# The first feature unit of two token groups by eight plain block products, half of the tokens at a time, with early loads

## Chip, cores, metric

One core of one Trainium2 chip. The metric is the device time of one execution in microseconds (us); lower is better. Ratios are the mean time of one kernel's fast runs over that of the other's fast runs of the same rounds, so not quite the ratio of the medians that are quoted beside them.

In the lines of the profile PE is TensorE's products, DVE is VectorE, ACT ScalarE, POOL GpSimd, and SPq the issue of a load. L315 is a line of that run's kernel file (each run has its own numbering), x8 a count of instructions. A wait reads: who waited <- for what: sum, times, longest (us). Of the tiles, `x` is the output of attention, `st` a state, `w` (before: `win`, `wout`) weights, `d` the banks of the plain products, `A_h` to `D_h` and `A_o` to `D_o` those of the hidden and the output products.

## The reference

```python
# attention: B=4, H=8, S=768, D=64; gamma_h = 1 - 2^(-5-h)
for t in range(S):
    state = gamma * state + outer(k[:, :, t], v[:, :, t])
    y[:, :, t] = q[:, :, t] @ state / sqrt(D)
# bridge: (B,H,S,D) -> x of 3072 tokens x 512
h = x @ w_in                      # 512 x 2048, float64 weights
out = maximum(0.01 * h, h) @ w_out    # 2048 x 512
```

The kernel handles the sequence in six groups `c` of 128 positions x 4 batches (512 tokens). Attention within a group is done by products (scores `ap`, masked `am`, values `yp`, state sums). The two large products use the seven-product scheme of Winograd on 2 x 2 blocks, over four "units" `u` of 512 hidden features. The weights come as float64 and are turned into float32 in 32 "pieces": ScalarE takes the powers, VectorE the mantissas.

## The kernel before

What the change and the argument touch (cuts marked):

```python
def sums(w):                     # weight sums of a unit: 4 VectorE operations
def differences(x, t):           # differences of x: 4 VectorE operations
...
PRODUCTS = {"M1": ("A", 0, 0), "M6": ("B", 5, 5), "M5": ("C", 4, 4), "M4": ("D", 3, 6),
            "M2": ("A", 2, 2), "M7": ("B", 1, 1), "M3": ("C", 6, 3)}
def seven(tiles, name, takes, order=...):   # 7 block products, each 4 matmuls
...                                         # (8 instructions in the trace)
load(0, 0); nc.sync.dma_start(out=dec, in_=decay)
load_piece(0); load_piece(1); load(0, 1); load_piece(2)
...                    # later heads are loaded into a ring of two, when the head two before is done
for b in range(B):                # group 0: four heads, then differences and sums
    scored(0, b)(); round_piece(); read(0, b)()
all_of(differences(*xs[0]), sums(win[0]))
for u in range(NU):
    for c in range(2):
        ...
        if (c, u) == (0, 0):      # two heads of group 1 beside group 0's products
            at = put(rounds(1), s0=[scored(1, 0)], s2=[read(1, 0)], s3=[scored(1, 1)], s5=[read(1, 1)])
        elif (c, u) == (1, 0):    # the other two with nothing beside them
            for b in range(2, B):
                scored(1, b)(); round_piece(); read(1, b)()
            differ(1)()
        run(hidden(c, u, *xs[c], *parts[c][1:], **order), at)
    for c in range(2):
        run(output(c, os[c], [parts[c]], u == 0, u == NU - 1), at)
```

Of the kernel before, what the change touches and what calls it, by code (L numbers as in the profile page):

```python
# [9 lines left out]
FP32 = mybir.dt.float32  # L10
# [8 lines left out]
C = 128  # L19
# [4 lines left out]
def kernel(  # L24
# [52 lines left out]

    win = [const.tile([128, 7, 2, 256], FP32, name=f"win{u}") for u in range(NU)]
    wout = [const.tile([128, 7, 2, 256], FP32, name=f"wout{u}") for u in range(NU - 1)]

    st = [const.tile([128, HP, D], FP32, name=f"st{b}") for b in range(B)]

    last_s4 = const.tile([128, 1, 2, 256], FP32, name="last_s4")
    if f64:
        last = []
    else:
        last = [const.tile([128, 2, 2, 256], FP32, name=f"last{h}") for h in range(3)]

    def block(w, i):

        if w is not last:
            return w[:, i]
        return w[i // 2][:, i % 2] if i < 6 else last_s4[:, 0]
# [9 lines left out]
    def load(c, b):  # L103
        x = work.tile([128, 2, HP, C], FP32, tag="qk", bufs=AHEAD, name=f"qk_{c}_{b}")
        y = work.tile([128, 2, H, D], FP32, tag="kv", bufs=AHEAD, name=f"kv_{c}_{b}")
        nc.sync.dma_start(out=x, in_=qk[c, b])
        nc.sync.dma_start(out=y, in_=kv[c, b])
        heads[c, b] = x, y
# [24 lines left out]
    def stage_y(c, bs, xb):  # L133
# [24 lines left out]
        for b, _, _, _, ps in got:  # L158
            th, o = divmod(b * C, N)
            blocks = xb.rearrange("p (kh th) k n -> p kh th k n", th=2)[:, :, th, :, ds(o, C)]  # L160
            nc.vector.tensor_tensor(out=blocks, in0=ps[:, :, 0 : HP // 2, :], in1=gq, op=ALU.mult)  # L161
            sp = sums[b]
            if more:
                if c > 0:
                    nc.vector.tensor_tensor(out=st[b], in0=st[b], in1=sp, op=ALU.add)
                nc.vector.tensor_tensor(out=st[b], in0=st[b] if c > 0 else sp,
                                        in1=gc.unsqueeze(2).to_broadcast([128, HP, D]),
                                        op=ALU.mult)
            n = c * B + b + AHEAD
            if n < NC * B and n - 2 * B not in range(AHEAD):  # L170
                load(*divmod(n, B))


    wout.append(last)
    units = [w for pair in zip(win, wout) for w in pair]
    N_PIECES = 4 * len(units)
    raws = {}
    done = [0]
# [4 lines left out]
    def piece(n):  # L183

        w, h, i = units[n // 4], n // 2 % 2, n % 2
        return w[h][:, :, i, :] if w is last else w[:, 2 * h : 2 * h + 2, i, :]

    def load_piece(n):
        if n >= N_PIECES:
            return  # L190
        if not f64:
            nc.sync.dma_start(out=piece(n), in_=weights[n].rearrange("p (h n) -> p h n", h=2))
            return
        tag, bufs = ("raw", 3) if n < N_PIECES - 4 else (("qk", "kv")[n % 2], AHEAD)
        raws[n] = work.tile([128, W], I64, tag=tag, bufs=bufs, name=f"raw{n}")
        nc.sync.dma_start(out=raws[n], in_=weights[n])

    def new_last(h):
        if f64 and len(last) == h:
            last.append(work.tile([128, 2, 2, 256], FP32, tag="raw", bufs=3, name=f"last{h}"))  # L200

    def round_piece():

        n = done[0]
        done[0] += 1
        if f64:
            mantissas(n)
        load_piece(n + 3)
        if n + 2 < N_PIECES and f64:
            powers(n + 2)  # L210
        if n == N_PIECES - 1:
            new_last(2)
            for b in range(AHEAD):
                load(2, b)
        if n % 4 == 3 and n > 3:
            all_of(sums(units[n // 4]))
# [3 lines left out]
    def powers(n):  # L220




        if n >= N_PIECES - 4:
            new_last(n // 2 % 2)
        top = raws[n].bitcast(U16).rearrange("p (h n four) -> p h n four", four=4, h=2)[:, :, :, 3]
        z = zs[n] = work.tile([128, 2, W // 2], I16, tag="z", bufs=3, name=f"z{n}")
        x = piece(n)


        nc.scalar.activation(x, top, AF.Prelu, alpha=float(BEND), scale=1.0 / 16,
                             bias=-7.5 / 16 - TOP)
        nc.scalar.activation(z, x, AF.Prelu, alpha=1.0 / BEND, bias=-float(BEND))
        nc.scalar.activation(z.bitcast(U16), z, AF.Relu, scale=128.0, bias=32768.0)
# [21 lines left out]
    def sums(w):  # L257

        a11, a21, a12, a22, s1, s2, s4 = (block(w, i) for i in range(7))
        plus(s1, a21, a22)  # L260
        yield
        minus(s2, s1, a11)
        yield
        minus(a21, a11, a21)
        yield
        minus(s4, a12, s2)
        yield

    def differences(x, t):

        minus(t[:, 0], x[:, 1], x[:, 0])
        yield
        minus(t[:, 1], x[:, 3], t[:, 0])
        yield
        minus(t[:, 2], x[:, 2], t[:, 1])
        yield
        minus(x[:, 1], x[:, 3], x[:, 1])
        yield

    def all_of(*steps):  # L280

        for _ in zip(*steps):
            pass


    PRODUCTS = {"M1": ("A", 0, 0), "M6": ("B", 5, 5), "M5": ("C", 4, 4), "M4": ("D", 3, 6),
                "M2": ("A", 2, 2), "M7": ("B", 1, 1), "M3": ("C", 6, 3)}

    def seven(tiles, name, takes, order=("M1", "M6", "M5", "M4", "M2", "M7", "M3")):
# [3 lines left out]
        for m in order:  # L293
            bank, sa, sb = PRODUCTS[m]
# [18 lines left out]
    def hidden(c, u, x, t, g, gd, **order):  # L313
# [6 lines left out]
        def takes(m, ps):  # L320
# [20 lines left out]
            elif m == "M3":  # L341
                plus(g[:, 1], got["u2"], ps)
                leaky(1)
                all_of(differences(g, gd))

        return seven([(win[u], x, t)], f"h{at}", takes, **order)

    def output(c, o, parts, first, final):
# [45 lines left out]
        return seven([(wout[u], g, gd) for u, g, gd in parts], f"o{at}", takes)  # L394


    def new_x(c):
        x = work.tile([128, 4, 2, N], FP32, tag="x", bufs=2, name=f"x_{c}")
# [30 lines left out]
    def differ(c):  # L429
        return lambda: all_of(differences(*xs[c]))  # L430
# [12 lines left out]
    load_piece(0)  # L443
    load_piece(1)
    load(0, 1)
    load_piece(2)
# [3 lines left out]
    if f64:  # L450
        powers(0)
        powers(1)

    xs = {}
    os = {}
    xs[0] = new_x(0)
    for b in range(B):
        scored(0, b)()
        round_piece()
        read(0, b)()  # L460
    all_of(differences(*xs[0]), sums(win[0]))


    for u in range(NU):
        parts = []
        for c in range(2):
            parts.append(new_g(c, u))
            order = {}
            at = rounds(1, 3)
            if (c, u) == (0, 0):  # L470
                xs[1] = new_x(1)
                order["order"] = ("M1", "M2", "M6", "M5", "M4", "M7", "M3")
                at = put(rounds(1), s0=[scored(1, 0)], s2=[read(1, 0)], s3=[scored(1, 1)],
                         s5=[read(1, 1)])
            elif (c, u) == (1, 0):
                for b in range(2, B):
                    scored(1, b)()
                    round_piece()
                    read(1, b)()
                differ(1)()  # L480
                at = rounds(1)
            run(hidden(c, u, *xs[c], *parts[c][1:], **order), at)
        for c in range(2):
            if u == 0:
                os[c] = new_o(c)
            at = rounds(1, 4) if u < NU - 1 else {}
            if u == NU - 1 and NC > 2:
# [106 lines left out]
```

## Time and profile before

| | before |
|---|---|
| time, median of 3 (range) | 686.09 us (685.8 to 687.5) |
| profiled execution | span 683.2 us, mean granted TensorE clock 0.995 |
| TensorE busy | 660.3 us, 97% |
| first output product (`A_o`) starts | 74.7 us in the chain |
| TensorE waits in the first 110 us / after | 18.7 us / none |

The lines are in the prediction below. The table is to be read as follows: after the first output product TensorE never waits, so a change in the opening is worth what it moves that start by, and no more.

### The profile page before, as it was taken

How to read it: one execution, taken by the hardware profiler on the slowest of the kernel's cores; microseconds unless marked ns; L12 is line 12 of the kernel's file. 1: busy time of each engine (PE TensorE's matmuls, PEld its weight loads, DVE VectorE, ACT ScalarE, POOL GpSimd, SP SyncE). 2: the span in 40 equal slices, each digit the busy share in tenths (PEclk: the TensorE clock that was granted, in tenths of full speed). 3: DMA queues.
4: the chain of work that ended last, by engine and by line, in shares of the span. 5: the costliest groups of instructions: out<-in, count | busy, mean ns of one | idle time of the engine just before them, and what ended most of it. 6: DMA issues, size and time to landing. Idle time of an engine off the chain costs nothing.

```text
span 683.2 us, 9545 instructions
## 1 busy us (share of the span) xinstructions
PE 660.3 (97%) x4096; PEld 577.8 (85%) x4096; DVE 375.9 (55%) x573; ACT 166.4 (24%) x275; POOL 27.4 (4%) x29
## 2 busy tenths in 40 slices
PE   5787999999999999999999999999999999999997
PEld 5666888888888888888888888888888888888886
DVE  4878767988888765613653533553451354341342
ACT  5422444445543001311210221220221130221210
POOL 1110000000001010100100100100000000000000
PEclk9998999999999999999999999999999999999999
DMA  8741212223412353100301300301300000100001
GB/s 317 284 155 62 86 69 88 91 69 123 153 33 93 127 181 117 71 1 12 112 1 62 124 0 1 124 1 62 124 0 1 1 1 16 46 1 0 1 1 62
DMA packets 15162, 49.12 MB, mean 72 GB/s; under 512 B 1680, under 2 KB 1680, under 8 KB 15120
## 3 DMA queue, kind: packets, MB, share of 16 engines
q1 hardware_dynamic: 15120, 48.51, 20.4%
q8 instruction: 32, 0.52, 0.3%
q14 instruction: 10, 0.08, 0.0%
HBM read 42.21 MB, written 6.29 MB: 71 GB/s over the span
## 4 chain that ended last, share of the span: by engine, by line
PE 94%; DMA 2%; DVE 1%; issue 1%; POOL 0%; SPq 0%; POOLq 0%
PE B_h L303 12%; PE A_o L303 12%; PE B_o L303 12%; PE C_o L303 12%; PE C_h L303 12%; PE A_h L303 12%; PE D_h L303 6%; PE D_o L303 6%; PE ap L126 3%; PE yp L148 3%; PE yp L143 1%; PE yp L155 1%; DMA qk<-in_qk_dram 1%; DMA dec<-decay_dram 1%; DMA kv<-in_kv_dram 1%
## 5 line engine op out<-in xcount | busy, mean ns | idle before, releaser
L303 PE MATMUL A_h<-x,win 128*128 128x256 f32 x384 | 91.0, 380 | 0.0
L303 PEld LDWEIGHTS A_h<-x,win 128*128 128x128 f32 x384 | 72.7, 190 | 10.0
L303 PE MATMUL A_o<-g,wout 128*128 128x256 f32 x288 | 68.2, 380 | 0.0
L318 ACT ACTIVATE g<-g 128x512 f32<-128x512 f32 x72 | 43.8, 630 | 85.3 <-DVE g L252 85.3
L303 PEld LDWEIGHTS A_o<-g,wout 128*128 128x128 f32 x288 | 54.6, 190 | 7.8 <-ACT g L333 0.5
L252 DVE TENSOR_TENSOR m<-m,B_h 128x512 f32<-128x512 f32 x24 | 16.5, 686 | 62.3 <-PE B_h L303 62.3
L323 ACT COPY m<-A_h 128x512 f32<-128x512 f32 x24 | 14.0, 582 | 136.5 <-PE A_h L303 104.1
L252 DVE TENSOR_TENSOR m<-m,B_o 128x512 f32<-128x512 f32 x16 | 11.0, 686 | 65.7 <-PE B_o L303 65.7
L303 PE MATMUL B_h<-t,win 128*128 128x256 f32 x192 | 45.5, 380 | 1.0 <-DVE t L255 1.0
L303 PE MATMUL C_h<-t,win 128*128 128x256 f32 x192 | 46.1, 383 | 0.0
L303 PE MATMUL B_h<-x,win 128*128 128x256 f32 x192 | 46.0, 382 | 0.0
L112 POOL TENSOR_TENSOR kv<-kv,dec 128x512 f32<-128x512 f32 x24 | 26.9, 1122 | 468.1 <-DMA kv<-in_kv_dram 241.0
L303 PE MATMUL D_h<-t,win 128*128 128x256 f32 x192 | 45.5, 380 | 0.0
L303 PE MATMUL C_h<-x,win 128*128 128x256 f32 x192 | 45.5, 380 | 0.0
L161 DVE TENSOR_TENSOR x<-yp,dec 128x512 f32<-128x512 f32 x24 | 16.5, 687 | 48.6 <-PE yp L155 36.3
L303 PEld LDWEIGHTS B_h<-t,win 128*128 128x128 f32 x192 | 36.4, 190 | 6.3 <-DVE t L255 1.4
L303 PEld LDWEIGHTS D_h<-t,win 128*128 128x128 f32 x192 | 36.4, 190 | 5.0
L303 PEld LDWEIGHTS C_h<-x,win 128*128 128x128 f32 x192 | 36.4, 190 | 5.0
L303 PEld LDWEIGHTS C_h<-t,win 128*128 128x128 f32 x192 | 35.9, 190 | 5.4
L303 PEld LDWEIGHTS B_h<-x,win 128*128 128x128 f32 x192 | 36.0, 190 | 5.3 <-issue 0.3
L148 PE MATMUL yp<-am,kv 128*64 128x128 f32 x384 | 27.1, 295 | 11.5 <-issue 7.3
L255 DVE TENSOR_TENSOR gd<-g,gd 128x512 f32<-128x512 f32 x48 | 36.4, 758 | 1.6
(88 smaller groups left out, 1004.3 us busy)
## 6 DMA issues: line engine op xcount, KB each, us to landing
raw<-in_weights_dram SPq DMA_DIRECT2D x32, 512.0 KB, 3.9
qk<-in_qk_dram SPq DMA_DIRECT2D x24, 512.0 KB, 4.3
kv<-in_kv_dram SPq DMA_DIRECT2D x24, 512.0 KB, 5.5
out_dram<-o SPq DMA_DIRECT2D x24, 256.0 KB, 2.1
dec<-decay_dram SPq DMA_DIRECT2D x1, 262.0 KB, 5.0
```

The source lines that it names most:

```text
L112: nc.gpsimd.tensor_tensor(out=v, in0=v, in1=gk.unsqueeze(2).to_broadcast([128, H, D]), op=ALU.mult)
L126: nc.tensor.matmul(ps[:, j, a, :], lhsT=x[ts(j, 64), 1, a, :], rhs=x[ts(j, 64), 0, a, :])
L143: nc.tensor.matmul(ps[ts(i, 64), j, m, :], lhsT=st[b][ts(j, 64), a, :], rhs=x[ts(j, 64), 0, a, :], start=(m == 0), stop=False, skip_group_ ...
L148: nc.tensor.matmul(ps[ts(i, 64), j, m, :], lhsT=y[:, 1, 2 * a + j, :], rhs=am[:, j, a, :], start=(c == 0 and m == 0), stop=True, skip_grou ...
L155: nc.tensor.matmul(sp[ts(j, 64), a, :], lhsT=y[:, 0, 2 * a + j, :], rhs=y[:, 1, 2 * a + j, :], start=False, stop=True, skip_group_check=True)
L161: nc.vector.tensor_tensor(out=blocks, in0=ps[:, :, 0 : HP // 2, :], in1=gq, op=ALU.mult)
L252: nc.vector.tensor_tensor(out=out, in0=a, in1=b, op=ALU.add)
L255: nc.vector.tensor_tensor(out=out, in0=a, in1=b, op=ALU.subtract)
L303: nc.tensor.matmul(ps[:, i, :], lhsT=block(w, sa)[:, k, ts(i, 128)], rhs=rhs[:, k, :], start=(first and i == 0 and n == 0 and k == 0), sto ...
L318: nc.scalar.activation(g[:, i], g[:, i], AF.Prelu, alpha=0.01)
L323: nc.scalar.copy(out=got["m1"], in_=ps)
```

## The change

Intent: with plain products a half of the tokens can start as soon as its two heads and two weight pieces are there, without sums of weights or differences of x. More heads are loaded from the start, into tiles whose own contents come later. Core of the diff:

```diff
+    def direct(c, u, x, g, th):          # 8 products of a group, in two halves of tokens th
+        banks = [psum.tile(...) for r in range(2)]
+        for kh in range(2):
+            for r in range(2):
+                for i in range(2):
+                    for k in range(2):
+                        nc.tensor.matmul(banks[r][:, i, :],
+                            lhsT=block(2 * u, r + 2 * kh)[:, k, ts(i, 128)],
+                            rhs=x[:, 2 * kh + th, k, :], ...)
+                if kh == 1:
+                    nc.scalar.activation(g[:, 2 * r + th], banks[r], AF.Prelu, alpha=0.01)
+                yield
...
+    load_piece(3, tile_x("words")...)
+    load(0, 2, new_o("in2"))
+    load(0, 3, new_o("in3"))
+    load(1, 0, unit_tile(LATE[2], "in10"))
+    load(1, 1, unit_tile(LATE[1], "in11"))
...
-    for b in range(B):
-        scored(0, b)()
-        round_piece()
-        read(0, b)()
-    all_of(differences(*xs[0]), sums(win[0]))
+    scored(0, 0)(); read(0, 0)(); scored(0, 1)(); next_mantissas(); next_powers()   # lines joined, some calls left out
+    read(0, 1)(); next_mantissas()
+    run(direct(0, 0, ..., 0), {1: [next_mantissas, next_mantissas, scored(0, 2)], 3: [scored(0, 3)]})
+    load(1, 2, unit_tile(LATE[0], "in12")); load(1, 3)
+    read(0, 2)(); read(0, 3)()
+    run(direct(0, 0, ..., 1), {1: [scored(1, 0)], 3: [scored(1, 1)]})
+    read(1, 0, 1)(); next_mantissas(); next_mantissas()
+    run(direct(1, 0, ..., 0), {1: [scored(1, 2)], 3: [scored(1, 3)]})
+    differences(*parts[0][1:]); read(1, 2, 3)(); next_mantissas()
+    run(direct(1, 0, ..., 1), {0: [next_mantissas]})
...
+            if u == 0:                        # moved: differences of x, weight sums of unit 0
+                put(at, s2=[differ(c)])
+                if c == 0:
+                    put(at, s3=[lambda: add_sums(0)])
```

I call the four calls of `direct` the half groups A, B (group 0) and C, D (group 1).

More of the change, by code (lines that the diff above doesn't have):

```diff
@@ L75, with unit_tile, new_pair, unit @@
     dec = const.tile([128, HP * C + H + HP], FP32, name="dec")
-    win = [const.tile([128, 7, 2, 256], FP32, name=f"win{u}") for u in range(NU)]
-    wout = [const.tile([128, 7, 2, 256], FP32, name=f"wout{u}") for u in range(NU - 1)]
     st = [const.tile([128, HP, D], FP32, name=f"st{b}") for b in range(B)]
+    units = {}
+    N_UNITS = 2 * NU
+    LATE = range(N_UNITS // 2, N_UNITS - 1)
     last_s4 = const.tile([128, 1, 2, 256], FP32, name="last_s4")
-    if f64:
-        last = []
-    else:
-        last = [const.tile([128, 2, 2, 256], FP32, name=f"last{h}") for h in range(3)]
-    def block(w, i):
-        if w is not last:
-            return w[:, i]
-        return w[i // 2][:, i % 2] if i < 6 else last_s4[:, 0]
+    def unit_tile(k, name):
+        if k in LATE:
+            return work.tile([128, 7, 2, 256], FP32, tag=f"late{k}", name=name)
+        return const.tile([128, 7, 2, 256], FP32, name=name)
+    def new_pair(h):
+        pairs = units.setdefault(N_UNITS - 1, [])
+        if len(pairs) == h:
+            pairs.append(work.tile([128, 2, 2, 256], FP32, tag="raw", bufs=3, name=f"last{h}"))
+    def unit(k):
+        if k not in units:
+            units[k] = unit_tile(k, f"w{k}")
+        return units[k]
+    def block(k, i):
+        if k < N_UNITS - 1:
+            return unit(k)[:, i]
+        return units[k][i // 2][:, i % 2] if i < 6 else last_s4[:, 0]
     gq = dec[:, 0 : HP * C].rearrange("p (j m t) -> p j m t", j=2, t=C)
@@ L101, with load @@
     AHEAD = 2
-    def load(c, b):
-        x = work.tile([128, 2, HP, C], FP32, tag="qk", bufs=AHEAD, name=f"qk_{c}_{b}")
-        y = work.tile([128, 2, H, D], FP32, tag="kv", bufs=AHEAD, name=f"kv_{c}_{b}")
+    def load(c, b, place=None):
+        if place is None:
+            x = work.tile([128, 2, HP, C], FP32, tag="qk", bufs=AHEAD, name=f"qk_{c}_{b}")
+            y = work.tile([128, 2, H, D], FP32, tag="kv", bufs=AHEAD, name=f"kv_{c}_{b}")
+        else:
+            flat = place.rearrange("p i k n -> p (i k n)")
+            half = 2 * HP * C
+            x = flat[:, 0:half].rearrange("p (s a t) -> p s a t", s=2, a=HP)
+            y = flat[:, half : 2 * half].rearrange("p (s h d) -> p s h d", s=2, h=H)
         nc.sync.dma_start(out=x, in_=qk[c, b])
@@ L169, in stage_y @@
             n = c * B + b + AHEAD
-            if n < NC * B and n - 2 * B not in range(AHEAD):
+            if c > 1 and n < NC * B:
                 load(*divmod(n, B))
-    wout.append(last)
-    units = [w for pair in zip(win, wout) for w in pair]
-    N_PIECES = 4 * len(units)
+    N_PIECES = 4 * N_UNITS
     raws = {}
-    done = [0]
+    done = {"powers": 0, "mantissas": 0}
     TOP = 1151
@@ L183, in piece, with load_piece @@
     def piece(n):
-        w, h, i = units[n // 4], n // 2 % 2, n % 2
-        return w[h][:, :, i, :] if w is last else w[:, 2 * h : 2 * h + 2, i, :]
-    def load_piece(n):
+        k, h, i = n // 4, n // 2 % 2, n % 2
+        if k < N_UNITS - 1:
+            return unit(k)[:, 2 * h : 2 * h + 2, i, :]
+        new_pair(h)
+        return units[k][h][:, :, i, :]
+    def load_piece(n, place=None):
         if n >= N_PIECES:
@@ L193, in load_piece, with next_powers, next_mantissas @@
             return
-        tag, bufs = ("raw", 3) if n < N_PIECES - 4 else (("qk", "kv")[n % 2], AHEAD)
-        raws[n] = work.tile([128, W], I64, tag=tag, bufs=bufs, name=f"raw{n}")
-        nc.sync.dma_start(out=raws[n], in_=weights[n])
-    def new_last(h):
-        if f64 and len(last) == h:
-            last.append(work.tile([128, 2, 2, 256], FP32, tag="raw", bufs=3, name=f"last{h}"))
-    def round_piece():
-        n = done[0]
-        done[0] += 1
+        if place is None:
+            tag, bufs = ("raw", 3) if n < N_PIECES - 4 else (("qk", "kv")[n % 2], AHEAD)
+            raws[n] = work.tile([128, W], I64, tag=tag, bufs=bufs, name=f"raw{n}")
+        else:
+            raws[n] = place.bitcast(I64)
+        nc.sync.dma_start(out=raws[n], in_=weights[n])
+    def next_powers():
+        n = done["powers"]
+        done["powers"] += 1
+        if n < N_PIECES and f64:
+            powers(n)
+    def next_mantissas():
+        n = done["mantissas"]
+        done["mantissas"] += 1
         if f64:
             mantissas(n)
-        load_piece(n + 3)
-        if n + 2 < N_PIECES and f64:
-            powers(n + 2)
+        if n != 3:
+            load_piece(n + 4 if n < 3 else n + 3)
         if n == N_PIECES - 1:
-            new_last(2)
+            new_pair(2)
             for b in range(AHEAD):
@@ L215, in round_piece @@
         if n % 4 == 3 and n > 3:
-            all_of(sums(units[n // 4]))
+            add_sums(n // 4)
+    def round_piece():
+        next_mantissas()
+        next_powers()
     zs = {}
     def powers(n):
-        if n >= N_PIECES - 4:
-            new_last(n // 2 % 2)
         top = raws[n].bitcast(U16).rearrange("p (h n four) -> p h n four", four=4, h=2)[:, :, :, 3]
@@ L255, in minus, with add_sums, seven @@
         nc.vector.tensor_tensor(out=out, in0=a, in1=b, op=ALU.subtract)
-    def sums(w):
-        a11, a21, a12, a22, s1, s2, s4 = (block(w, i) for i in range(7))
+    def add_sums(k):
+        a11, a21, a12, a22, s1, s2, s4 = (block(k, i) for i in range(7))
         plus(s1, a21, a22)
-        yield
+        minus(a21, a11, a21)
         minus(s2, s1, a11)
-        yield
-        minus(a21, a11, a21)
-        yield
         minus(s4, a12, s2)
-        yield
     def differences(x, t):
         minus(t[:, 0], x[:, 1], x[:, 0])
-        yield
         minus(t[:, 1], x[:, 3], t[:, 0])
-        yield
         minus(t[:, 2], x[:, 2], t[:, 1])
-        yield
         minus(x[:, 1], x[:, 3], x[:, 1])
-        yield
-    def all_of(*steps):
-        for _ in zip(*steps):
-            pass
-    PRODUCTS = {"M1": ("A", 0, 0), "M6": ("B", 5, 5), "M5": ("C", 4, 4), "M4": ("D", 3, 6),
-                "M2": ("A", 2, 2), "M7": ("B", 1, 1), "M3": ("C", 6, 3)}
-    def seven(tiles, name, takes, order=("M1", "M6", "M5", "M4", "M2", "M7", "M3")):
+    def seven(tiles, name, takes):
         banks = {}
-        for m in order:
-            bank, sa, sb = PRODUCTS[m]
+        which = [("M1", "A", 0, 0), ("M6", "B", 5, 5), ("M5", "C", 4, 4), ("M4", "D", 3, 6),
+                 ("M2", "A", 2, 2), ("M7", "B", 1, 1), ("M3", "C", 6, 3)]
+        for m, bank, sa, sb in which:
             first = bank not in banks
@@ L311, in temp, with hidden @@
         return work.tile([128, 2, N], FP32, tag=name, name=f"{name}_{at}")
-    def hidden(c, u, x, t, g, gd, **order):
+    def direct(c, u, x, g, th):
+        banks = [psum.tile([128, 2, N], FP32, tag="ff", bufs=4, name=f"d{r}_{c}_{th}")
+                 for r in range(2)]
+        for kh in range(2):
+            for r in range(2):
+                for i in range(2):
+                    for k in range(2):
+                        nc.tensor.matmul(
+                            banks[r][:, i, :], lhsT=block(2 * u, r + 2 * kh)[:, k, ts(i, 128)],
+                            rhs=x[:, 2 * kh + th, k, :], start=(kh == 0 and i == 0 and k == 0),
+                            stop=(kh == 1 and k == 1), skip_group_check=True)
+                if kh == 1:
+                    nc.scalar.activation(g[:, 2 * r + th], banks[r], AF.Prelu, alpha=0.01)
+                yield
+    def hidden(c, u, x, t, g, gd):
         got = {}
@@ L343, in takes @@
                 leaky(1)
-                all_of(differences(g, gd))
-        return seven([(win[u], x, t)], f"h{at}", takes, **order)
+                differences(g, gd)
+        return seven([(2 * u, x, t)], f"h{at}", takes)
     def output(c, o, parts, first, final):
@@ L392, in takes, with tile_x @@
                 store(1)
-        return seven([(wout[u], g, gd) for u, g, gd in parts], f"o{at}", takes)
+        return seven([(2 * u + 1, g, gd) for u, g, gd in parts], f"o{at}", takes)
+    def tile_x(c):
+        return work.tile([128, 4, 2, N], FP32, tag="x", bufs=2, name=f"x_{c}")
     def new_x(c):
-        x = work.tile([128, 4, 2, N], FP32, tag="x", bufs=2, name=f"x_{c}")
+        x = tile_x(c)
         t = work.tile([128, 3, 2, N], FP32, tag="t", bufs=2, name=f"t_{c}")
@@ L429, in differ @@
     def differ(c):
-        return lambda: all_of(differences(*xs[c]))
+        return lambda: differences(*xs[c])
     def put(at, **more):
@@ L442 @@
     nc.sync.dma_start(out=dec, in_=decay)
-    load_piece(0)
-    load_piece(1)
     load(0, 1)
-    load_piece(2)
+    for n in range(3):
+        load_piece(n)
+    load_piece(3, tile_x("words").rearrange("p i k n -> p (i k n)")[:, 0 : 2 * W])
+    load(0, 2, new_o("in2"))
+    load(0, 3, new_o("in3"))
+    load(1, 0, unit_tile(LATE[2], "in10"))
+    load(1, 1, unit_tile(LATE[1], "in11"))
     nc.vector.memset(mask, 1.0)
@@ L449 @@
                             base=0, pattern=[[1, 128]], channel_multiplier=-1)
-    if f64:
-        powers(0)
-        powers(1)
-    xs = {}
+    for _ in range(3):
+        next_powers()
+    xs = {0: new_x(0)}
     os = {}
-    xs[0] = new_x(0)
-    for b in range(B):
-        scored(0, b)()
-        round_piece()
-        read(0, b)()
-    all_of(differences(*xs[0]), sums(win[0]))
+    parts = [new_g(0, 0)]
+    scored(0, 0)()
+    read(0, 0)()
+    scored(0, 1)()
+    next_mantissas()
+    next_powers()
+    read(0, 1)()
+    next_mantissas()
+    run(direct(0, 0, xs[0][0], parts[0][1], 0),
+        {1: [next_mantissas, next_mantissas, scored(0, 2)], 3: [scored(0, 3)]})
+    load(1, 2, unit_tile(LATE[0], "in12"))
+    load(1, 3)
+    read(0, 2)()
+    read(0, 3)()
+    run(direct(0, 0, xs[0][0], parts[0][1], 1), {1: [scored(1, 0)], 3: [scored(1, 1)]})
+    next_powers()
+    next_powers()
+    xs[1] = new_x(1)
+    parts.append(new_g(1, 0))
+    read(1, 0, 1)()
+    next_mantissas()
+    next_mantissas()
+    run(direct(1, 0, xs[1][0], parts[1][1], 0), {1: [scored(1, 2)], 3: [scored(1, 3)]})
+    next_powers()
+    next_powers()
+    differences(*parts[0][1:])
+    read(1, 2, 3)()
+    next_mantissas()
+    run(direct(1, 0, xs[1][0], parts[1][1], 1), {0: [next_mantissas]})
+    next_powers()
+    next_powers()
+    differences(*parts[1][1:])
     for u in range(NU):
-        parts = []
-        for c in range(2):
+        for c in range(2) if u > 0 else ():
+            if c == 0:
+                parts = []
             parts.append(new_g(c, u))
-            order = {}
-            at = rounds(1, 3)
-            if (c, u) == (0, 0):
-                xs[1] = new_x(1)
-                order["order"] = ("M1", "M2", "M6", "M5", "M4", "M7", "M3")
-                at = put(rounds(1), s0=[scored(1, 0)], s2=[read(1, 0)], s3=[scored(1, 1)],
-                         s5=[read(1, 1)])
-            elif (c, u) == (1, 0):
-                for b in range(2, B):
-                    scored(1, b)()
-                    round_piece()
-                    read(1, b)()
-                differ(1)()
-                at = rounds(1)
-            run(hidden(c, u, *xs[c], *parts[c][1:], **order), at)
+            run(hidden(c, u, *xs[c], *parts[c][1:]), rounds(1, 3))
         for c in range(2):
@@ L486 @@
             at = rounds(1, 4) if u < NU - 1 else {}
+            if u == 0:
+                put(at, s2=[differ(c)])
+                if c == 0:
+                    put(at, s3=[lambda: add_sums(0)])
             if u == NU - 1 and NC > 2:
```

## The prediction

The sum: -1.9 for the start, the moved work and GpSimd, then +0.5 and -0.4, which gives 684.3 us. What is left after the first cut ("the fall", "the return", "the start was slow") is about the granted clock in the profile of the kernel before.

> **What bounds the kernel now.** I read the page first (engine totals and the rows of 40 slices), then TensorE's waits before and after 110 us, then the chain that ended last and the timeline of the first 110 us, then tables by stretch. The page:
>
> ```profile
> PE 660.3 (97%) x4096; PEld 577.8 (85%) x4096; DVE 375.9 (55%) x573; ACT 166.4 (24%) x275; POOL 27.4 (4%) x29
> PE   5787999999999999999999999999999999999997
> ```
>
> TensorE is busy 97% of the span, and each digit covers 17 us: only the first four or five are below 9. So 22.9 us (683.2 less 660.3) are idle, nearly all at the start. The list of TensorE's waits between 110 us and the end is empty; that of the first 110 us holds five rows, sum 18.7 us:
>
> ```profile
> PE yp L148 <- issue: 7.3, 4, 4.6
> PE ap L126 <- DMA qk<-in_qk_dram: 6.2, 3, 4.6
> PE yp L148 <- DVE am L129: 2.7, 2, 1.4
> PE yp L148 <- POOL kv L112: 1.5, 1, 1.5
> PE B_h L303 <- DVE t L255: 1.0, 1, 1.0
> ```
>
> 4.6 us of it is the first load. The rest, 14.1 us, is the attention products waiting for inputs or for VectorE. Idle is not the whole loss. In the chain (start, duration, what) the same work takes two durations:
>
> ```profile
> 8.14 1.97 PE yp L148 x16
> 10.11 0.85 PE yp L155 x16
> 10.97 2.03 PE ap L126 x16
> ...
> 25.35 1.09 PE yp L148 x16
> 26.45 0.47 PE yp L155 x16
> 26.91 1.92 PE A_h L303 x8
> 28.83 1.09 PE ap L126 x16
> ...
> 33.58 0.60 PE yp L143 x16
> ...
> 53.42 1.97 PE yp L148 x16
> ...
> 74.72 1.73 PE A_o L303 x8
> ```
>
> Up to about 17 us and again from 53.4 to 58 us TensorE runs at half speed. The table by stretch shows why in the second case (the number after POOL's is the granted clock):
>
> ```profile
> 49.00:50.00 1.00, 0.00 (x0) 0.00 (x0) 0.97 (x2) 0.94 (x3) 0.00 (x0) 1.00 0.05 20
> 51.00:52.00 1.00, 0.00 (x0) 0.00 (x0) 1.00 (x1) 0.00 (x0) 0.64 (x1) 0.84 0.00 0
> 53.00:54.00 1.00, 0.58 (x6) 0.61 (x8) 0.97 (x3) 0.00 (x0) 0.00 (x0) 0.50 0.00 0
> 58.00:59.00 1.00, 0.98 (x20) 0.56 (x16) 0.69 (x1) 0.97 (x2) 0.00 (x0) 0.74 0.00 0
> ```
>
> TensorE stops at 48.9, the clock falls to half at about 51.7 (after 2.8 us), work resumes at 53.4 and full clock is back at about 58.5.
>
> Everything after the first output product, which starts at 74.5 us, is back-to-back TensorE work, and apart from moved VectorE work it is the same in both kernels. So **the question is only when the first output product can start.** Budget at full clock up to it: group 0 attention 4 x (1.09 + 1.09 + 0.47) = 10.6; group 1, with the state product, 4 x (1.09 + 0.60 + 1.09 + 0.47) = 13.0; seven products of eight instructions for two groups, 2 x 7 x 1.73 = 24.2. Sum 47.8, against 74.5 - 4.6 = 69.9 us elapsed: **22.1 us lost**, of which 14.1 idle, 6.6 half clock (three score products of +0.94, three value products of +0.88, three state sums of +0.38), and the rest re-entry: a first product after a small one takes 1.92, not 1.73.
>
> [...] here the fall came after 2.8 us of idle and the return after 5.1 us of work, and the start was slow for 12 us. [...] a VectorE subtraction beside the GpSimd scaling of v (50.28 to 51.64) takes 1.53 us instead of 0.68:
>
> ```profile
> 50.28 1.36 POOL L112 TENSOR_TENSOR kv<-kv,dec 128x512 f32<-128x512 f32 x1 [5.76 <-DMA kv<-in_kv_dram]
> 50.65 1.53 DVE L255 TENSOR_TENSOR g<-g 128x512 f32<-128x512 f32 x1
> ```
>
> [...] The trace shows 421 GB/s between 8 and 12 us, with all loads queued; later the rate falls to 52 to 186 GB/s by stretch as loads wait for a free buffer.
>
> **The change part by part.**
>
> *Added products.* Eight block products per group in place of seven: 2 x 1.73 = **3.5 us** more TensorE time that nothing hides (TensorE 4096 to 4112 instructions). No other engine can pay for it, so the ceiling of the gain is 22.1 - 3.5 = 18.6 us, and the slow start (4.5 us) and the wait for the decay table stay.
>
> *Inputs early.* Loads for four more heads go to tiles not yet in use, so they wait for nothing. At about 1.33 us per 512 KB (4.6 us first landing, 6.5 transfers more by 13.3 us) I estimate: weight pieces 0 to 3 at 10.7, 12.0, 13.4, 14.7; group 0 all in by 20.1; the first half of group 1 by 25.4; the rest by 35. Each is ahead of its use. This removes the DMA waits after the first (1.6 us) and the 4.6 us wait at 48.9, with the half clock it caused (about 2.3 us).
>
> *VectorE.* The direct form has no sums to make after products: 2 x 5 operations of about 0.66 us pitch go (6.6 us), and 4 copies on ScalarE. The differences of x for both groups and the weight sums of unit 0 (12 operations, 8 us) move into the two output stages.
>
> *The new chain on TensorE*, using the durations above (us from start). Scores and values of head 0: 4.6 to 10.96, head 1: 10.97 to 17.1, as before. Mask, then piece 0's mantissas fit before; x of head 1 at 17.2 to 17.85, its state to 18.3, then piece 1's mantissas (1.85) to 20.1. The direct products need both pieces: **TensorE idles 17.1 to 20.1 but for 0.4.** Then by halves: 1.92 + 1.73, score 1.09, 1.92 + 1.73, score 1.1: 29.35 (VectorE finishes pieces 2 and 3 near 24 to 25, at about the time they are wanted). Values of heads 2 and 3, the second waiting for its mask: 32.45; x of head 3: 33.15 (0.7 idle). Second half: 33.15 + 7.3 + two scores 2.2 = 42.65. Pair read of group 1: mask wait 0.7 in between, then 0.55 + 1.90 + 0.93: 47.3; then x and state of both heads on VectorE, 48.95 (1.7 idle). Again 7.3 + 2.2 = 58.5; pair read 63.15; x to 64.85 (1.7 idle); the last half, with no score in it, 1.92 + 3 x 1.73 = 7.1: **first output product at 72.0**, against 74.5. GpSimd's scaling collides with pieces 2 and 3; I add 0.3. So the losses after the change, in order: 1.4 decay table, 4.5 slow clock, 1.4 mask, 2.6 piece 1, 0.7 + 0.7 + 1.7 + 0.7 + 1.7 in the reads, re-entries 1.4. The waits by DMA are traded for waits by VectorE's short chains, since one half of tokens has little else to run beside it.
>
> *Moved VectorE work.* From 72: differences of g to +2.8, then one sum (4.3), a weight piece (6.1), differences of x (8.8), weight sums (11.4), a piece (13.2), three sums (15.1), one (15.7). The next stage wants its second bank at 13.8 and its third at 15.6: freed at 13.8 and 15.7. So VectorE is just full in these 24 us; stall 0 to 0.6, I take 0.3.
>
> *Sum:* -2.5 + 0.3 + 0.3 = -1.9. The 3 us gap at 17 to 20 us is as long as the idle that halved the clock at 51.7; I give a second half-clock episode (about 2 us) a chance of one in four, 0.5. On the other side my estimates of VectorE's order are in places late (nothing lets me check them), worth 0.4. **686.1 - 1.8 = 684.3 us.**
>
> **The rivals.** (a) *Waits replaced less fully than I think*, so the gain is most of what was idle: full 14.1 idle less the slow-start parts leaves about 8 after the 3.5 are paid: 678. For it: all inputs come early. Against: five of my gaps are dependence chains (mask, x, state) that no early load shortens. (b) *VectorE becomes the bound* at the outputs and at pieces 1 to 3, or the clock falls in the 17 to 20 gap: the gain is eaten, 686 to 688. For it: the rows of VectorE are at 9.2 to 11.1 busy of 12.1 us in the stages up to 220 us, so a debt is paid back slowly. (c) *It is hidden anyway*: the 3.5 us of extra products equal what is won, 686.
>
> **Range and chances.** (a) alone gives the low end, (b) the high: 80% between 680.5 and 687.3. Over 2% faster would need the first output at 61 us, with 11 us less loss than I count: 0.03. Over 2% slower needs a second stall of the same size: 0.02. Within 2%: 0.95.
>
> **What would show it.** Right: 4112 matmuls; no DMA wait of TensorE after 5 us; a gap of 2 to 3 us by VectorE on a weight piece near 18 us; waits of 1 to 2 us on x before each direct half of group 1; first output product at 71 to 73.5; VectorE over 11 of 12.1 us in both output stages of unit 0; no row by stretch at clock 0.50. Wrong: a clock of 0.50 after 20 us, the first output product before 69 or after 75, or stalls on PSUM between 72 and 110.

## The result

683.9 us median (683.35 to 684.47, 4 runs) against 686.8 us (685.8 to 688.02, 4 runs) in the same rounds: ratio 0.9957, 95% interval 0.9936 to 0.9978, so the same within 2%. The profiled execution has a span of 682.1 us.

The page after, engine totals and TensorE in 40 slices:

```profile
PE 661.7 (97%) x4112; PEld 577.8 (85%) x4112; DVE 369.2 (54%) x563; ACT 162.2 (24%) x271; POOL 27.2 (4%) x29
PE   5888999999999999999999999999999999999997
```

The 16 instructions of the eighth products are there. TensorE's waits in the first 110 us after the change (sum, times, longest):

```profile
PE d L333 <- DVE x L182: 5.2, 4, 1.8
PE ap L147 <- DMA qk<-in_qk_dram: 4.6, 1, 4.6
PE d L333 <- DVE w L276: 2.1, 1, 2.1
PE yp L169 <- POOL kv L133: 1.6, 1, 1.6
PE yp L164 <- DVE am L150: 1.5, 2, 0.7
PE yp L169 <- issue: 1.4, 1, 1.4
PE B_h L315 <- DVE w L283: 0.3, 1, 0.3
```

DMA is gone but for the first load. What remains, 16.7 us in all against 18.7, is led by VectorE: x, a weight piece (w), masks. The chain (start, duration, what):

```profile
8.30 1.98 PE yp L169 x16
...
15.90 0.68 DVE x L182
...
19.48 4.85 PE d L333 x14
...
25.42 3.65 PE d L333 x16
...
66.21 7.15 PE d L333 x32
73.35 1.73 PE A_o L315 x8
```

The first output product starts at 73.35, against 74.72. The 14 instructions from 19.48 take 4.85 us where 16 of the same take 3.65 at 25.42. The table by stretch (granted clock after POOL's count) says why:

```profile
18.00:19.00 1.00, 0.00 (x0) 0.00 (x0) 0.92 (x1) 0.64 (x2) 0.88 (x1) 1.00 1.07 418
19.00:20.00 1.00, 0.52 (x1) 0.50 (x2) 0.97 (x3) 0.00 (x0) 0.00 (x0) 0.63 1.00 389
20.00:21.00 1.00, 1.00 (x4) 0.76 (x3) 0.90 (x2) 0.00 (x0) 0.00 (x0) 0.50 1.01 410
22.00:24.00 2.00, 2.00 (x9) 1.61 (x8) 1.76 (x2) 0.00 (x0) 0.58 (x2) 0.83 1.02 408
```

In the gap before weight piece 1 the clock fell to half at about 19.3 and came back at about 22.7.

### The profile page after: what moved, and what is told of

Same layout as the page of the kernel before. It is cut to its first block, busy times and chain, and to the rows that moved or that the text cites. A ratio compares the mean times of both kernels' runs of the same rounds, so it can differ in the third digit from the quotient of the medians.

```text
span 682.1 us, 9555 instructions
## 1 busy us (share of the span) xinstructions
PE 661.7 (97%) x4112; PEld 577.8 (85%) x4112; DVE 369.2 (54%) x563; ACT 162.2 (24%) x271; POOL 27.2 (4%) x29
## 3 DMA queue, kind: packets, MB, share of 16 engines
q1 hardware_dynamic: 15120, 48.51, 20.2%
## 4 chain that ended last, share of the span: by engine, by line
PE 95%; DVE 3%; DMA 1%; issue 0%; POOL 0%; SPq 0%; DVEq 0%; POOLq 0%
PE A_o L315 12%; PE B_o L315 12%; PE C_o L315 12%; PE B_h L315 11%; PE C_h L315 11%; PE A_h L315 11%; PE D_o L315 6%; PE D_h L315 6%; PE d L333 4%; PE ap L147 4%; PE yp L169 3%; PE yp L164 1%; PE yp L176 1%; DMA dec<-decay_dram 1%; DVE x L182 1%; DVE w L276 0%
## 5 line engine op out<-in xcount | busy, mean ns | idle before, releaser
L315 PE MATMUL A_h<-x,w 128*128 128x256 f32 x352 | 83.2, 379 | 0.0
L315 PEld LDWEIGHTS A_h<-x,w 128*128 128x128 f32 x352 | 66.9, 190 | 9.1
L315 PE MATMUL A_o<-g,w 128*128 128x256 f32 x288 | 68.1, 379 | 0.0
L315 PEld LDWEIGHTS A_o<-g,w 128*128 128x128 f32 x288 | 54.6, 190 | 7.9 <-ACT g L361 0.4
L315 PE MATMUL C_h<-t,w 128*128 128x256 f32 x176 | 42.2, 383 | 0.0
L315 PE MATMUL B_h<-x,w 128*128 128x256 f32 x176 | 42.2, 383 | 0.0
L315 PE MATMUL B_h<-t,w 128*128 128x256 f32 x176 | 41.7, 379 | 0.3 <-DVE w L283 0.3
L315 PE MATMUL D_h<-t,w 128*128 128x256 f32 x176 | 41.6, 379 | 0.0
L315 PE MATMUL C_h<-x,w 128*128 128x256 f32 x176 | 41.6, 379 | 0.0
L315 PEld LDWEIGHTS B_h<-t,w 128*128 128x128 f32 x176 | 33.4, 190 | 5.2 <-issue 0.7
```

Of the source, the lines that this page charges most:

```text
L315: nc.tensor.matmul(ps[:, i, :], lhsT=block(w, sa)[:, k, ts(i, 128)], rhs=rhs[:, k, :], start=(first and i == 0 and n == 0 and k == 0), sto ...
```

## The experiments

Two theories stood at the start. **Mine:** the 3.5 us of the eighth products are paid in full; what is won is waiting, and what is left are short chains on VectorE that no load shortens, plus one stretch of half clock. **Rival:** the gain is the early loads (or the plain products) alone, and the other part is idle or harmful.

The first four ran on one chip against the same 11 executions of the kernel before (median 685.21, 683.38 to 688.74); the others on a second chip (11, then 12 executions, medians 686.23 and 686.37). A time is best compared inside its series. Where a few tenths matter I use the start of the first output product in the trace.

| run | median us (range) | ratio to before (95%) | first output product |
|---|---|---|---|
| e0_after | 684.49 (683.88 to 685.0) | 0.9985 (0.9963 to 1.0007) | 73.78 |
| e1_ring_loads | 684.84 (684.36 to 685.07) | 0.9991 (0.9969 to 1.0012) | 73.79 |
| e2_seven_early | 707.01 (703.82 to 709.49) | 1.0312 (1.0279 to 1.0345) | confounded |
| e3_filler | 684.08 (683.54 to 686.51) | 0.9987 (0.9963 to 1.0012) | 73.16 |
| e4_x_first | 683.40 (681.95 to 683.69) | 0.9957 (0.9937 to 0.9977) | 72.64 |
| e5_seven_early2 | 684.22 (683.01 to 687.85) | 0.9986 (0.9958 to 1.0014) | 77.96 |
| e7_seven_of_eight | 682.31 (679.36 to 683.14) | 0.9942 (0.9917 to 0.9967) | 70.47 |
| e6_beside | 674.11, four fast (one more at 1793.52) | 0.9834 (0.9809 to 0.9858) | see e6_again |
| e6_again | 675.00 (674.07 to 677.11) | 0.9845 (0.9821 to 0.9869) | 64.81 |
| e8_opening | 674.41 (674.0 to 675.17) | 0.9832 (0.9809 to 0.9855) | 65.31 |
| e9_sums_late | 683.64 (683.51 to 685.76) | 0.9972 (0.9948 to 0.9997) | 73.76 |
| e10_filler4 | 683.48 (683.14 to 685.13) | 0.9967 (0.9945 to 0.9989) | 72.74 |

**e0_after: the changed kernel once more.** No edit.

> The changed kernel once more, as the yardstick of this series. Expected 683.9 us, ratio to the kernel before 0.9957. Theory: the first output product at about 73.2 us and one stretch of half clock near 19 to 23 us. Rival (the half clock there was chance of that one execution[...]): another execution shows a different stretch or none.

As expected in the trace (half clock from about 20.2 to 23.6). The ratio to before is nearer to 1 in this series, and its interval includes 1: the kernel before scatters by 5 us, the changed one by 1.

**e1_ring_loads: without the early loads.**

```diff
-    load(0, 2, new_o("in2")) ... load(1, 1, unit_tile(LATE[1], "in11"))
+    load(0, 2) after read(0, 0); load(0, 3) after read(0, 1); load(1, 0) after read(0, 2); ...
```

> The changed kernel with the inputs of four heads in the two-deep ring again (each load waits for the head two before it). Theory (after the change TensorE waits for VectorE's chains, and each half group gives a load 5 us or more): within 0.7 us of the changed kernel, that is 683.5 to 684.6, with at most 1 us of TensorE waits by DMA after the first load. Rival (the early inputs are the gain): back to the kernel before or worse, 686 to 690, with waits by DMA of 3 us and more.

0.35 us above e0 in the median, first output product at the same time, and no DMA wait but the first, of 4.7 us. With half groups in this order, each ring load has time enough. The early loads of heads add nothing measurable to the plain products.

**e2_seven_early: early loads, seven products.** The opening of before (four heads, then `hidden` with seven products in before's order) on the early loads; ScalarE's powers ran three pieces ahead.

> The other half alone: early inputs, but seven products and the order of work of the kernel before. Theory (the eighth product costs 3.5 us and pays itself by its better order, a gain of a few us): the early inputs alone give what the second and third head waited for data, 1.6 us, and the collision of GpSimd and VectorE at 50 us, 0.9 us: 683.5 to 685.0, with the wait before the values of head 2 of group 1 still 3 to 4.5 us because VectorE makes differences of g first. Rival (the plain products are the gain): no better than the kernel before, 686. Second rival (early inputs are all): 4 us and more below the changed kernel, since no 3.5 us are paid: 680 or less.

A miss of the experiment. The cause is in TensorE's waits, first 140 us of e2:

```profile
PE A_h L317 <- ACT m L353: 4.6, 1, 4.6
PE C_h L317 <- ACT m L359: 4.0, 3, 2.0
```

ScalarE had started on weight pieces whose loads were queued behind the early inputs, and the copies of the products (`m`) came only after those pieces: in the chain such a load takes 10.1 us (23.5 to 33.6), ScalarE works on pieces from 33.65 to 37.53, then makes the copy, and `A_h` starts at 38.06. The two rows are 8.6 of some 22 us lost; the granted clock was below full in six of the twelve stretches up to 140 us (0.67 to 0.94; mean of the run 0.980 against 0.997 in e0). It says nothing on the theories, but it shows a price of early loads: what was queued behind them came later. With the early loads of the change, too, the weight pieces of the first 40 us took 7.7 to 11.5 us from issue to landing (median 9.5); in the first 70 us of the kernel before they took 3.2 to 9.0 (median 5.5).

**e5_seven_early2: the same, mended.**

```diff
-        scored(0, b)(); round_piece(); read(0, b)()        # powers 3 ahead
+        scored(0, b)(); next_mantissas(); read(0, b)()     # next_powers only for b == 0
...
+    s0=[scored(1, 0), next_powers, next_powers]            # after the first product's copy
...                         # loads of heads 2 and 3 of group 1: now after group 0's heads
```

> The early inputs with seven products once more, mended: the earlier form let ScalarE start on weight pieces that were still queued behind the early inputs[...]. Now ScalarE takes pieces 4 and 5 after the first product's copy. Theory (early inputs alone are worth 2.5 us at most, as the values of head 2 of group 1 still wait for VectorE): 683 to 685.5, with one wait of 3 to 4.5 us near 48 us and half clock after it. Rival one (no gain without the plain products): 686 or more. Rival two (early inputs alone are better): below 681.

Four executions are at 683.0 to 684.8, two at 687.7 and 687.9; the profiled one is of the slower kind. Its longest wait of TensorE, and the engines in the gap near 54 us (the third busy time is VectorE's, the last two numbers are DMA's):

```profile
PE yp L169 <- issue: 9.8, 5, 3.7
```

```profile
54.00:55.00 1.00, 0.00 (x0) 0.00 (x0) 0.97 (x3) 0.53 (x1) 0.00 (x0) 1.00 0.00 0
```

The wait of 3.7 us is there as expected, while VectorE is busy throughout and no load runs: it was never a wait for data alone. The clock was half from 55.2 to 62.0. Early loads alone give a median of 684.2, plain products alone (e1) 684.8, both (e0) 684.5. The series differ, so no ranking follows, and all three intervals include 1: against the kernel before, none of the three shows a gain clear of noise. That the two parts are substitutes and not a sum fits these times (each alone comes to what both give), but is not shown. The traces do show that e1 starts its first output product when e0 does. That of e5 starts 4.2 us later, but in an execution of its slower kind.

**e7_seven_of_eight: what the eighth product costs.** Wrong result (relative error 0.068).

```diff
-                    for k in range(2):
+                    for k in range(2) if (kh, r, i) != (1, 1, 1) else ():
```

> Wrong result on purpose: the changed kernel with four of 32 products of each group left out (an eighth), everything else in place. Theory (nothing hides the eighth product; a term of 3.5 us): first output product 3.0 to 3.5 us earlier and time 2.5 to 3.5 us below the changed kernel, 681 to 682. Rival (TensorE waits for VectorE so much in these half groups that the extra product is hidden): less than 1.5 us.

The start of the first output product in e0, then in e7:

```profile
73.78 1.73 PE A_o L315 x8
70.47 1.73 PE A_o L315 x8
```

It comes 3.3 us earlier (3.4 when counted from the start of half group A, 19.77 and 19.90): the term of 3.5 us is right, and nothing hides it. The profiled span is 3.0 us shorter than e0's (679.6 against 682.6). The median fell less, 1.3 to 2.2 us (against e9 on the same chip and e0), which I cannot trace as the other executions have no profile.

**e3_filler and e10_filler4: the half clock.** Products of constants, never read, laid between the values of head 1 and half group A; seven in e3, four in e10.

```diff
+    filler = psum.tile([128, 2, N], FP32, tag="ff", bufs=4, name="filler")
+    for _ in range(7):            # 4 in e10
+        nc.tensor.matmul(filler[:, 0, :], lhsT=mask, rhs=dec[:, 0:N], start=True, stop=True, ...)
```

> The changed kernel with seven products of constants (result unread) laid into TensorE's gap at 16 to 19 us. They need 3 us that TensorE idles in any case. Theory (the idle gap halved the clock, and the half clock cost 1.4 us in the first four direct blocks): no stretch at 0.50 there, the first half of the first direct products in about 3.5 us instead of 4.9, time 1.0 to 1.5 us below the changed kernel, 682.5. Rival (the clock has another cause, or the half clock is hidden by the weight pieces 2 and 3 on VectorE): time unchanged within 0.4 us, or longer.

> The filler of e3 cut from seven products of constants to four. Seven took 3.35 us and ran past the time at which piece 1 was ready, so they gave back about 1 us of what the full clock won. Theory: no half clock after 17 us, first half of the first direct products 3.5 us from 19.4 to 19.9, first output product at 72.2 to 72.6 (changed kernel 73.35 and 73.8), time 1.0 to 1.5 us below it, 682.5 to 683.4. Rival (a filler this short leaves an idle stretch in which the clock falls as before): half clock again, time as the changed kernel.

Both remove the half clock (recorded mean clock 0.999 to 1.000 in all their executions, 0.997 in e0's but one). In the chain of e10:

```profile
20.12 3.29 PE d L333 x14
```

The same 14 instructions take 3.29 us instead of 4.85 to 4.98, **1.6 us for the half clock**, and the first output product comes 1.0 us before e0's. In e3 the slow opening lasted longer (the values of head 1 took 1.98 us at 14.48, where e0's took 1.09 at 14.42), the seven fillers ended at 20.66 and ran past piece 1; what was won was 0.6. The time follows only in part: e3 is 0.4 us below e0, unclear, and e10 0.2 us below its nearest neighbour e9. In e3 the trace shows the give-back. The larger of its two TensorE waits after 73 us:

```profile
PE A_o L315 <- ACT g L361: 1.2, 2, 1.0
```

The row lies at 120 to 172 us. The chain of the larger wait runs: mantissas on VectorE (from 165.6), load of a new piece into the freed tile (166.3 to 169.5), powers on ScalarE (169.5 to 171.5), and only then the activation that the next output product needs, which starts at 172.0. The expected 1.0 to 1.5 us was thus right for the stage and too much for the total.

**e4_x_first: the order of x and states on VectorE.**

```diff
         for b, _, _, _, ps in got:
             ...
             nc.vector.tensor_tensor(out=blocks, in0=ps[:, :, 0 : HP // 2, :], in1=gq, op=ALU.mult)
+        for b, _, _, _, ps in got:
             sp = sums[b]
```

> The changed kernel with one edit: in a read of two heads VectorE writes x of both before it updates their states. Theory (the 1.8 us waits before both half groups of group 1 are the chain x, state, state, x on VectorE, no load could shorten them): these two waits fall to about 0.9 us each, first output product 1.7 us earlier, time 1.0 to 1.7 us below the changed kernel, 682.8 to 683.5. Rival (something else ends those waits, or the time is given back later): waits or time unchanged within 0.4 us.

The waits on x fall from 5.2 to 3.6 us, the longest from 1.8 to 1.0:

```profile
PE d L334 <- DVE x L182: 3.6, 4, 1.0
```

First output product 1.1 us before e0's although half group A started 0.4 later here. The waits are the chain named. Of the time, 0.2 us (against e9) to 1.1 us (against e0) is seen.

**e9_sums_late: VectorE work moved on.** The weight sums of unit 0 go from the first output stage to the last unit's.

```diff
-                if c == 0:
-                    put(at, s3=[lambda: add_sums(0)])
...
+                if c == 0:
+                    put(at, s5=[lambda: add_sums(0)])      # at the last unit
```

> The changed kernel with one edit: the four weight sums of unit 0 move from the first output stage to the last unit's. Theory (moved VectorE work makes the 0.3 us wait of a hidden product at about 100 us): that wait is gone, time lower by 0.3 us, 683.5 to 684.3. Rival (the wait has another cause): the wait stays.

The list of TensorE's waits after 74 us is empty in e9, so the 0.3 us wait did come from VectorE's load. In time, 0.3 us is below what these rounds resolve.

**e6_beside and e6_again: work laid beside the chains.** Same products and loads as the change.

```diff
-    run(direct(0, 0, ..., 0), {1: [next_mantissas, next_mantissas, scored(0, 2)], 3: [scored(0, 3)]})
-    read(0, 2)(); read(0, 3)()
-    run(direct(0, 0, ..., 1), {1: [scored(1, 0)], 3: [scored(1, 1)]})
-    read(1, 0, 1)()
+    decay_v(0, 2); stage_p(0, 2); next_mantissas()            # scores of head 2 into the gap
+    run(direct(0, 0, ..., 0), {0: [next_mantissas, lambda: stage_m(0, 2), next_mantissas],
+                               1: [scored(0, 3)], 2: [read(0, 2, 3)]})
+    run(direct(0, 0, ..., 1), {0: [scored(1, 0), next_powers, next_powers],
+                               1: [scored(1, 1)], 2: [read(1, 0, 1)]})
     ...                            # half group C likewise; e4's and e9's edits too
```

> A version built on the theory that what is left are VectorE's chains with nothing of TensorE's beside them: scores are laid after the first two blocks of each half group, the read of the next heads before its last block, x of both heads before the states, the scores of head 2 into the gap at 17 us, and the weight sums of unit 0 move to the last unit. Same products and same loads. Theory: first output product at 65 to 67 us instead of 73.8, waits of TensorE on x and on masks after 20 us under 1.5 us in total, no half clock after 20 us, time 676 to 679. Rival (moved VectorE work and the weight pipeline behind it give it back later): first output product early but time over 681, with waits of TensorE after 70 us of 3 us and more.

> The same kernel as e6_beside, since one of its five executions, the profiled one, took 1793 us with every product some 2.8 times as long and no wait added. Theory (a state of the chip in that one execution, not of the kernel): no execution over 680 us, median 674 to 676, first output product at 65 to 67 us, waits of TensorE on x and masks after 20 us under 1.5 us. Rival (the kernel brings it on): again at least one execution over 1000 us.

675.0 us, ratio 0.9845 (0.9821 to 0.9869): 1.6% below the kernel before, and under the changed kernel by 8.6 us against e9, 9.5 against e0. TensorE's waits of e6_again in the first 74 us, and the start of its first output product:

```profile
PE ap L148 <- DMA qk<-in_qk_dram: 5.1, 1, 5.1
PE yp L173 <- POOL kv L133: 1.4, 1, 1.4
PE yp L173 <- issue: 1.4, 1, 1.4
PE d L338 <- DVE w L281: 1.2, 1, 1.2
PE ap L148 <- DMA o_in<-in_qk_dram: 0.7, 1, 0.7
```

```profile
64.81 1.73 PE A_o L320 x8
```

All waits for x and masks after 20 us are gone; nothing is given back after 74 us, where the list of waits is empty. e6 makes several edits at once, so its gain is split by the waits only: in e0 the waits on x and masks were 6.7 us and the half clock cost 1.6, which is 8.3 of the 9.0 us by which the first output product comes earlier. The mean clock is 1.000 here; two of six executions had 0.997.

One execution of e6_beside, the profiled one, took 1793 us. Its products were slow throughout (a group of eight block-product instructions 4.86 us instead of 1.73), and no wait was added. Its trace holds no record of the clock at all, so the 1.00 that the views print for it says nothing (they print 1.00 also for the first 17.5 us of the kernel before, where its trace has no record and the same products take 1.97 us that later take 1.09). None of the other ten executions of the same kernel (four of the first set, six of the second) did this. I count it as a state of that execution; its cause stays open.

**e8_opening: the first 17 us.** On e6, scores of heads 0 and 1 before the values of head 0, with both `qk` loaded first.

```diff
-    scored(0, 0)(); read(0, 0)(); scored(0, 1)()
+    scored(0, 0)(); scored(0, 1)(); read(0, 0)()
```

> e6 with the scores of heads 0 and 1 both before the values of head 0, and their qk loaded first, so that the mask of head 1 and the decay table are waited for beside work. Theory (the waits of 1.4 and 1.4 us at 7 and 13 us are on the path): 1.0 to 2.3 us below e6, 672 to 673.5. Rival (piece 1 of the weights sets the start of the first direct products, whatever comes before): within 0.5 us of e6, with a longer wait on the weight piece near 17 us.

No gain over e6, in the trace (first output product at 65.31 against 64.81) or in the time. The longest of TensorE's waits after the first load:

```profile
PE ap L150 <- DMA o_in<-in_qk_dram: 3.7, 1, 3.7
```

The values of head 1 end at 12.5 instead of 15.6, but the next scores need head 2, which lands at 16.1; with the idle of 3.7 us the clock is half from 14.7 to 21.5. The wait has moved to DMA, neither to the weight piece, as the rival said, nor away.

## Why the prediction was right

The time, 684.3 predicted and 683.9 measured, agrees closely; step by step it agrees less well, and the close fit is in part luck, since two errors cancel.

- **The eighth products, 3.5 us, unhidden:** right. 3.3 us by leaving them out (e7), and 16 more instructions.
- **DMA waits vanish, VectorE's chains take their place:** right. The four gaps before the half groups were foretold as 2.6, 0.7, 1.7, 1.7; the trace shows 3.0 (0.9 on x and 2.1 on the weight piece), 0.8, 1.8, 1.8. e4 shortened the last two by the edit that only the named chain answers to. But the step credited this to the early loads; e1 shows that the order of the half groups alone does it. The prediction had not asked what a ring of two would still achieve.
- **The first output product at 72.0 plus 0.3, measured 73.35:** the term that failed is the half clock in the gap at 17 to 20 us, given a chance of one in four at 2 us. It came in all six profiled executions of kernels with that gap (the result's, e0, e1, e4, e7, e9), and cost 1.6 us (e10). The opening's own slow stretch ended earlier in that execution, x of head 1 at 15.9 and not 17.2, which gave back 0.6. Against 72.0 about 0.4 us remain; two handovers of 0.14 us from VectorE to TensorE (at 49.92 and 66.07), which the working left out, are part of them. The 0.3 set aside for GpSimd beside pieces 2 and 3 was not needed: piece 3 was ready at 23.9, the products that use it began at 25.42. Collisions were seen: one mantissa operation of piece 1 took 1.34 us (at 18.08) and one of piece 3 took 1.41 us (at 21.66) beside GpSimd's scaling (17.44 to 18.88, 21.38 to 22.53); without it the same operations of piece 2 took 0.69 us each (at 20.59 and 19.80).
- **VectorE's debt in the output stages, 0.3 us:** right in size (0.3 us at 99.7 us). It showed as a hidden product waiting for the weight sums of the second feature unit, not as a PSUM bank held too long. VectorE was 9.5 and 11.5 us busy of 12.1 in the two stages; "over 11 in both" was wrong for the first.
- **The signs.** Apart from that one, one sign of being right failed, "no row by stretch at clock 0.50", and one sign of being wrong came true: a clock of 0.50 after 20 us (until 22.7). The mechanism was right except for the clock and for what was credited to the early loads.
- **Slips in reading and adding.** The chain shown has the first output product at 74.72, not 74.5. Of the 22.9 us idle, 4.2 lie behind TensorE's last product and not at the start. One of VectorE's stages up to 220 us has 6.7 us busy, below "9.2 to 11.1". The terms that lead to 29.35 add to 29.6 (29.2 if the 0.4 done earlier is taken off), and the listed losses to 16.8, where 72.0 leaves 16.1. None moves the sum by more than 0.7.
- **Where the two errors cancel.** The profiles differ by only 1.4 us at the first output product and 1.1 us in span, the medians by 2.9. The profile of before was of a favourable execution: clock 0.995, as its one stretch of 6.8 us at half clock makes it (the slow opening has no clock record and is not in the mean; by the same sum 0.990 would be some 14 us, an estimate). Over the 23 later executions of the kernel before, the seven with a mean clock of 0.994 and more average 684.7 us, the 16 below that 686.3. The changed kernel has 0.997 in the four executions of the result and a time within 1.1 us. So a good part of the measured gain may be that the changed kernel escapes the longer stretches of half clock that the kernel before falls into, more often than not; that is a correlation over executions, not an experiment. At the fastest, the two kernels meet: 683.38 against 683.35 us (different series). The prediction took the losses of one profile and subtracted from a median.
- **The rivals.** Rival (c), "the extra products equal what is won", is the nearest to the truth for executions at a high clock. The second half of rival (b) came true, the clock fell in the gap, but it cost 1.6 us and not the whole gain; VectorE did not become the bound. Rival (a), a gain of 8 us, failed as the change stood, for the reason given; e6 shows that those 8 us were there, behind the order of work.

So the change moved little for two reasons. By the chain, the loss before the first output product fell from 22.3 us (74.72 less 4.6 and less 47.8 of work) to about 17.4 (73.35 less 4.6 and less 51.3), and 3.5 of these 4.9 us went into the eighth products. And the plain products were not yet laid beside the chains that feed them, which e6 shows to be worth about 9 us. Open are the scatter of the kernel before, as far as it is only correlated with the clock, the part of e7's and e10's earlier start that the times do not show, and the one execution of 1793 us.

## What to carry to other kernels

A finer grain of work (half groups) removed waits for data here (TensorE's on DMA: 6.2 us before, 4.6 after), but each grain brought its own chain of mask, x and state; the gain came when that chain was put beside the last block of the grain before, as in e6, not from the grain itself. Before paying products for earlier starts, ask which engine ends the wait: a gap of 4.6 us here looked like a late load and was mostly VectorE's order of work. An idle gap on TensorE cost more here than its length: in all six profiles with the gap before half group A (2.3 to 3.2 us idle) the clock fell at its end or just after (at 19.3 to 20.5 us), worth 1.6 us, while after the gaps of 1.8 us before C and D it stayed full. And where executions scatter, look at the granted clock of each before reading a difference of medians.
